# Layer two's weights converted earlier, and bits hashed in four row groups, in a hash attention and two-layer feed-forward kernel

## The chip, the cores and the metric

The kernel runs on one core of a Trainium2 chip. Its time is the device time of one execution in microseconds (us). The engines are TensorE (PE in the profile; its weight loads are PEld), VectorE (DVE), ScalarE (ACT), GpSimd (POOL) and SyncE (SP), which here issues every transfer. They run at the same time and wait for each other through semaphores; each takes its own instructions strictly in the order in which they were written out when the kernel was built.

## What is computed

Attention in which a query sees only keys of its own bucket, then two feed-forward layers on the result:

```python
q_bits = (einsum('bhsd,dk->bhsk', q, proj) > 0)          # 6 bits, k_bits likewise
mask = q_bucket[:, :, :, None] == k_bucket[:, :, None, :]
scores = where(mask, q @ k.T / sqrt(D), -1e9)            # B 2, H 8, S 768, D 64
x = softmax(scores) @ v                                  # as 1536 tokens of 512
x = relu(x @ w_in)**2 @ w_out                            # layer one, 512 -> 2048 -> 512
h = x @ w_in2
out = (max(h, 0) + alpha * min(h, 0)) @ w_out2           # layer two
```

The four weight matrices come as float64, and reach the core as pairs of 32-bit words.

## The kernel before

The 1536 tokens are cut into four chunks (c = 0 to 3) of 384. A chunk's attention is four pairs of heads; a pair is six units (two heads by three blocks of 128 queries). Layer one runs `feed_forward(0, c)` and layer two `feed_forward(1, c)`, each over 16 blocks f of the hidden width. Attention of chunk 0 runs alone at the start; attention of chunk c + 1 is cut into steps that a `Background` object hands out between the matmuls of `feed_forward(0, c)` by a table of marks, so that it is done 0.8 of a chunk after chunk c began. Chunk 3 of layer one has no attention beside it.

*Weights.* A unit u = (layer, f, o) is one 128x512 block of the input (o = 0) or output (o = 1) weights. `load_bits` brings its 512 KB of words from DRAM (tile wbits). `to_f32` makes float32 of them with one ACT instruction (line 444, tile we) and three on DVE (446 and 447 to wsg, 448 to the result). `split_w` then splits a float32 block into a high part (wh, ACT, line 462) and the rest (wl, line 463, on DVE or POOL), and the matmuls use both. Layer one's 32 units are converted in `fetch`, and written to DRAM (`w_d`), during `feed_forward(0, 0)` and a little before; chunks 1 to 3 load them back as 256 KB each (tile wf, line 488). Layer two's 32 units are converted by `keep` into a pool that stays (`res`), by a `Background` whose marks spread them from the start of chunk 3 of layer one to 0.3 of the first chunk of layer two.

*Bits.* `hash_bits` multiplies a pair's keys (768 columns) or queries (384) by the projection, 128 columns wide, with float32 matmuls (line 214), and DVE takes the sign into tile bits (215). `matches` multiplies these by a table of +1 and -1 (`code`, line 227), so that equal buckets can be told from the sums.

*Key halves.* `k_split` rounds each head's 64 rows of keys to the matmul format on ACT (236), writes the remainder to the other 64 rows on DVE (237) and copies the rounded part to a second tile on POOL (238).

*Evictions.* `p_t` transposes the exponentials and copies them out of PSUM, 3 by 128 columns at a time, on ACT ("a", line 317) or DVE ("v", line 319) by the strings in `EVICT`, one per chunk. `scores` has the score matmuls (292, 293), a maximum on DVE (`low`, 296) and the exponential on ACT (`sm`, 299).

A scheduler writes out each engine's order at build time from the program's order and its own idea of durations; pools with one or two buffers decide what must wait for what.

## Time and profile before

| | |
|---|---|
| median of three runs | 870.07 us (867.12 to 870.68) |
| the profiled execution | 869.21 us, of which its span 867.4 us |
| mean granted TensorE clock | 0.985 of full speed |
| busy share: PE, DVE, ACT, POOL | 93%, 64%, 55%, 44% |
| moved by DMA | 96.40 MB |

The span runs from the first instruction to the last; 1.8 us lie around it. A busy PE can still be waiting inside an instruction, so its share says little by itself: what counts is the time that a stage takes against the matmuls it has to do. The stages follow from the copies of the chunk results out of PSUM: attention 0 runs to about 91 us (first matmul of layer one at 90.88), chunk 0 to 246, chunk 1 to 377, chunk 2 to 491, chunk 3 to 588, and the four chunks of layer two take 69 us each, and the last writes out its result.

### The profile page before, as it was taken

How to read it: one execution, taken by the hardware profiler on the slowest of the kernel's cores; microseconds unless marked ns; L12 is line 12 of the kernel's file. 1: busy time of each engine (PE TensorE's matmuls, PEld its weight loads, DVE VectorE, ACT ScalarE, POOL GpSimd, SP SyncE). 2: the span in 40 equal slices, each digit the busy share in tenths (PEclk: the TensorE clock that was granted, in tenths of full speed). 3: DMA queues.
4: the chain of work that ended last, by engine and by line, in shares of the span. 5: the costliest groups of instructions: out<-in, count | busy, mean ns of one | idle time of the engine just before them, and what ended most of it. 6: DMA issues, size and time to landing. Idle time of an engine off the chain costs nothing.

```text
span 867.4 us, 12076 instructions
## 1 busy us (share of the span) xinstructions
PE 810.9 (93%) x4192; PEld 653.4 (75%) x4192; DVE 552.7 (64%) x854; ACT 480.6 (55%) x925; POOL 378.6 (44%) x328
## 2 busy tenths in 40 slices
PE   5998998899999999999999998868999999999996
PEld 3655677676768778778777877647998998998995
DVE  6989899997666345366454599978445444444442
ACT  5668668776656556557555656654444444444331
POOL 3011233432646556433332554475555555554553
PEclk7999999999999999999999999989999999999999
DMA  7442766664332233342223777750010010000000
GB/s 232 139 133 96 254 183 210 223 203 133 112 129 71 88 110 80 89 126 85 71 82 88 274 234 259 262 215 37 1 37 37 0 38 37 1 1 37 1 0 37
DMA packets 42989, 96.40 MB, mean 111 GB/s; under 512 B 5200, under 2 KB 13744, under 8 KB 42928
## 3 DMA queue, kind: packets, MB, share of 16 engines
q1 hardware_dynamic: 42928, 95.63, 34.2%
q8 instruction: 33, 0.54, 0.3%
q14 instruction: 28, 0.23, 0.1%
HBM read 80.88 MB, written 14.73 MB: 110 GB/s over the span
## 4 chain that ended last, share of the span: by engine, by line
PE 59%; DVE 9%; issue 4%; ACT 3%; DMA 3%; POOL 2%; SPq 0%; POOLq 0%; DVEq 0%; ACTq 0%
PE acc L542 8%; PE acc L538 7%; PE acc L539 7%; PE m L329 5%; PE h L510 4%; PE h L512 4%; PE h L511 4%; PE m L313 4%; PE m L512 3%; PE m L510 3%; PE m L511 3%; PE s L292 2%; PE s L293 2%; DVE wsg L447 2%; DVE wl L463 2%
## 5 line engine op out<-in xcount | busy, mean ns | idle before, releaser
L528 POOL TENSOR_TENSOR gl<-g,gh 128x384 fp32r<-128x384 f32 x128 | 142.6, 1114 | 266.3 <-ACT gh L527 122.2
L538 PE MATMUL acc<-wh,gh 128*128 128x512 f32 x384 | 162.0, 422 | 12.6 <-ACT gh L519 10.2
L463 POOL TENSOR_TENSOR wl<-wf,wh 128x512 fp32r<-128x512 f32 x80 | 107.7, 1347 | 119.3 <-ACT wh L462 109.0
L539 PE MATMUL acc<-wl,gh 128*128 128x512 f32 x384 | 152.2, 396 | 0.0
L542 PE MATMUL acc<-wh,gl 128*128 128x512 f32 x384 | 117.2, 404 | 9.0 <-POOL gl L528 8.9
L462 ACT ACTIVATE wh<-w 128x512 fp32r<-128x512 f32 x128 | 80.4, 629 | 74.8 <-PE m L511 40.3
L462 ACT ACTIVATE wh<-wf 128x512 fp32r<-128x512 f32 x128 | 79.5, 627 | 56.0 <-PE h L511 28.9
L510 PE MATMUL h<-xh,wh 128*128 128x384 f32 x296 | 107.2, 362 | 1.1 <-ACT xh L357 0.8
L511 PE MATMUL h<-xl,wh 128*128 128x384 f32 x296 | 101.0, 341 | 0.6 <-POOL xl L358 0.6
L512 PE MATMUL h<-xh,wl 128*128 128x384 f32 x296 | 101.2, 342 | 0.0
L296 DVE TENSOR_REDUCE low<-s 128x1 f32<-128x768 f32 x84 | 80.1, 954 | 29.4 <-PE s L293 28.7
L538 PEld LDWEIGHTS acc<-wh,gh 128*128 128x128 f32 x384 | 72.6, 189 | 31.1 <-ACT gh L519 13.0
L542 PEld LDWEIGHTS acc<-wh,gl 128*128 128x128 f32 x384 | 71.9, 190 | 30.8 <-POOL gl L528 15.2
L299 ACT ACTIVATE sm<-s,low 128x768 f32<-128x768 f32 x84 | 75.3, 896 | 27.4 <-DVE low L296 27.1
L313 PE MATMUL m<-ident,sm 128*128 128x128 f32 x528 | 83.0, 274 | 5.8 <-DVE bits L215 4.0
L463 POOL TENSOR_TENSOR wl<-w,wh 128x512 fp32r<-128x512 f32 x64 | 83.9, 1310 | 8.9 <-ACT wh L462 8.6
L313 PEld LDWEIGHTS m<-ident,sm 128*128 128x128 f32 x528 | 65.5, 140 | 21.8 <-DVE bits L215 4.9
L539 PEld LDWEIGHTS acc<-wl,gh 128*128 128x128 f32 x384 | 72.9, 190 | 9.7 <-issue 1.2
L527 ACT ACTIVATE gh<-g 128x384 fp32r<-128x384 f32 x64 | 33.5, 524 | 83.6 <-DVE g L526 83.6
L525 DVE TENSOR_SCALAR r<-m,alpha_sb 128x384 f32<-128x384 f32 x43 | 26.5, 617 | 82.3 <-PE m L512 82.1
L319 DVE COPY pt<-m 128x384 f32<-128x384 f32 x112 | 61.4, 552 | 23.3 <-PE m L313 23.0
L512 PE MATMUL m<-xh,wl 128*128 128x384 f32 x216 | 72.9, 338 | 0.5 <-DVE wl L463 0.5
(105 smaller groups left out, 1568.6 us busy)
## 6 DMA issues: line engine op xcount, KB each, us to landing
wf<-w SPq DMA_DIRECT2D x96, 256.0 KB
wbits<-in_w_in_dram SPq DMA_DIRECT2D x32, 512.0 KB
wbits<-in_w_out_dram SPq DMA_DIRECT2D x32, 512.0 KB
w<-wf SPq DMA_DIRECT2D x32, 256.0 KB
qr<-in_qT_dram SPq DMA_DIRECT2D x32, 192.0 KB
kr<-in_kT_dram SPq DMA_DIRECT2D x8, 384.0 KB
qn<-in_qT_dram SPq DMA_DIRECT2D x16, 192.0 KB
vr<-in_v_dram SPq DMA_DIRECT2D x8, 384.0 KB
```

The lines of the kernel that those rows point to most:

```text
L296: nc.vector.tensor_reduce(low, ps[:, 0:2, 0:HALF], AX.XY, ALU.max, negate=True)
L299: nc.scalar.activation(sm.rearrange("p (a n) -> p a n", a=2), ps[:, 0:2, 0:HALF], AF.Exp, bias=low, accum_out=self.sums[:, i:i + 1],)
L313: nc.tensor.transpose(ps[:, i * P:(i + 1) * P], pp[:, b * P:(b + 1) * P], ident)
L462: nc.scalar.activation(hi, w, AF.Copy)
L463: engine.tensor_tensor(lo, w, f32(hi), ALU.subtract)
L510: nc.tensor.matmul(hp, wih[:, ks], xh[:, kk, :], start=first, stop=False)
L511: nc.tensor.matmul(hp, wih[:, ks], xl[:, kk, :], start=False, stop=False)
L512: nc.tensor.matmul(hp, wil[:, ks], xh[:, kk, :], start=False, stop=last)
L528: nc.gpsimd.tensor_tensor(gl, g, f32(gh), ALU.subtract)
L538: nc.tensor.matmul(acc[:, t, :], gh[:, blocks[t]], woh, start=first, stop=False)
L539: nc.tensor.matmul(acc[:, t, :], gh[:, blocks[t]], wol, start=False, stop=False)
L542: nc.tensor.matmul(acc[:, t, :], gl[:, blocks[t]], woh, start=False, stop=last)
```

## The change

Four edits come together.

*Layer two's conversion.* Its units are now converted in chunks 1 and 2 of layer one, by steps handed out from 1.0 to 2.9, beside the attention steps: `ahead` converts a unit in place in the tile we and stores it to DRAM. `keep` becomes a load of 256 KB from there, from 0.25 of chunk 3 to 0.3 of layer two's first chunk. The tiles we and wsg have one buffer in place of two in the later stage, and the tile pool of wf outlives the attention.

*Bits.* The projection keeps 16 columns per head (32 in all). `hash_bits` cuts the columns of keys or queries into four parts and multiplies each into its own group of 32 PSUM partitions, so DVE takes signs of 192 columns for keys and 96 for queries. `matches` uses one table per group, four matmuls and four weight loads per call. The tables take some more small instructions at the start.

*Key halves.* Except for the very first pair, POOL subtracts in place in the key tile, and two transfers per head move the rounded part to the second tile and the remainder to the other 64 rows.

*Evictions.* Chunk 0 and chunk 1 have one more "a" per head each, two per pair.

```diff
-EVICT = ("avavav", "vvavva", "vvavva", "vvavva")
+EVICT = ("aavaav", "avavav", "vvavva", "vvavva")
...
-        state["conv"] = pool(f"conv{late}", 1 + late, stack)
+        state["conv"] = pool(f"conv{late}", 1, stack)
...
+    GR = 32
+    NG = P // GR
-    proj_sb = const.tile([P, P], F32, name="proj_sb")
+    proj_sb = const.tile([P, 2, GR // 2], F32, name="proj_sb")
-    code = const.tile([P, P], BF16, name="code")
+    code = const.tile([P, NG, P], BF16, name="code")
...
         def hash_bits(self, x, n):
+            w = n // NG
+            bits = p1.tile([P, S // NG], BF16, tag="bits", name="bits")[:, 0:w]
+            ps = m_tile()
+            for g in range(NG):
+                nc.tensor.matmul(
+                    ps[g * GR:(g + 1) * GR, 0:w], proj_sb.rearrange("p h n -> p (h n)"), x[:, g * w:(g + 1) * w],
+                    start=True, stop=True,
+                )
+            nc.vector.tensor_scalar(bits, ps[:, 0:w], 0.0, None, ALU.is_gt)
+            return bits
...
-            for a in range(n // T):
-                nc.tensor.matmul(ps[:, a, 0:T], code, bits[:, a * T:(a + 1) * T], start=True, stop=True)
+            for g in range(NG):
+                a, k = divmod(g * w, T)
+                nc.tensor.matmul(ps[:, a, k:k + w], code[:, g, :], bits, start=True, stop=True)
...
+            shift = self.c > 0 or self.j > 0
             for h in range(2):
                 r, o = self.rows(h)
                 nc.scalar.activation(self.k1[r, h], self.kr[r], AF.Copy)
-                nc.vector.tensor_tensor(self.k1[o, h], self.kr[r], f32(self.k1[r, h]), ALU.subtract)
-                nc.gpsimd.tensor_copy(self.k2[r, h], f32(self.k1[r, h]))
+                if shift:
+                    nc.gpsimd.tensor_tensor(
+                        self.kr[r].bitcast(F32R), self.kr[r], f32(self.k1[r, h]), ALU.subtract
+                    )
+                    nc.sync.dma_start(out=f32(self.k2[r, h]), in_=f32(self.k1[r, h]))
+                    nc.sync.dma_start(out=f32(self.k1[o, h]), in_=self.kr[r])
...
+    def ahead(u):
+        w = to_f32(u)
+        w_d[u] = dram.tile([P, DM], F32, tag="w%d_%d_%d" % u, name="w%d_%d_%d" % u)
+        nc.sync.dma_start(out=w_d[u], in_=w)
+
     def keep(u):
         kept[u] = state["res"].tile([P, DM], F32, name="w%d_%d_%d" % u)
-        to_f32(u, kept[u])
+        nc.sync.dma_start(out=kept[u], in_=w_d[u])
...
+    for f in range(KFF):
+        for o in range(2):
+            steps += [lambda u=(1, f, o): load_bits(u), lambda u=(1, f, o): ahead(u)]
+    conversion = Background(steps, [(1.0, 0), (NCH - 1.1, len(steps))])
...
     steps = [lambda f=f, o=o: keep((1, f, o)) for f in range(KFF) for o in range(2)]
-    conversion = Background(steps, [(0.0, 0), (1.3, len(steps))])
+    conversion = Background(steps, [(0.25, 0), (1.3, len(steps))])
```

How the written order moves is shown at three places. Names end in a number that tells tiles apart; an arrow points from what is read to what is written.

DVE in chunk 3 of layer one, before (446 to 448 convert layer two's units, 463 splits a unit of layer one):

```order
L448 SCALAR_TENSOR_TENSOR w1_2_0_5528<-we_5531,wsg_5533 128x512
L446 TENSOR_SCALAR wsg_5551<-wbits_5547 128x512
L447 SCALAR_TENSOR_TENSOR wsg_5551<-wbits_5547,wsg_5551 128x512
L448 SCALAR_TENSOR_TENSOR w1_2_1_5546<-we_5549,wsg_5551 128x512
L463 TENSOR_TENSOR wl0_5607<-wf_5584,wh0_5606 128x512
L446 TENSOR_SCALAR wsg_5595<-wbits_5591 128x512
L447 SCALAR_TENSOR_TENSOR wsg_5595<-wbits_5591,wsg_5595 128x512
L448 SCALAR_TENSOR_TENSOR w1_3_0_5590<-we_5593,wsg_5595 128x512
```

DVE at the end of chunk 2 and in chunk 3, in the changed kernel (496 is the split, 556 the square of the hidden value, 625 the chunk's copy out, 652 part of the next layer's input):

```order
L556 TENSOR_TENSOR g_5709<-r_5708 128x384
L556 TENSOR_TENSOR g_5759<-r_5758 128x384
L625 COPY y_5788<-acc_4548 128x512 x2
L496 TENSOR_TENSOR wl0_5819<-wf_5766,wh0_5818 128x512
L496 TENSOR_TENSOR wl0_5852<-wf_5847,wh0_5851 128x512
L496 TENSOR_TENSOR wl0_5895<-wf_5880,wh0_5894 128x512
L652 TENSOR_TENSOR xl_6060<-s_6118,xh_6059 128x4x128
L496 TENSOR_TENSOR wl0_5937<-wf_5923,wh0_5936 128x512
```

None of the 29 conversions that stood in chunk 3 is left there.

DVE in chunk 1, before (a pair's reciprocals, evictions and signs):

```order
L341 RECIPROCAL rin_3794<-rin_3794 128x6
L319 COPY pt_3712<-m_3775 128x384
L319 COPY pt_3712<-m_3782 128x384
L345 COPY rrow_3799<-m_3797 6x128
L356 TENSOR_TENSOR x_3859<-u_3839,rb_3803 128x384
L215 TENSOR_SCALAR bits_3876<-m_3877 128x384
L296 TENSOR_REDUCE low_3901<-s_3896 128x1
L215 TENSOR_SCALAR bits_3935<-m_3936 128x384
```

and in the changed kernel, around the same work (471, 472 and 474 convert; 321 is the maximum, 344 the eviction, 232 the signs):

```order
L370 COPY rrow_3362<-m_3360 6x128
L474 SCALAR_TENSOR_TENSOR we_3773<-we_3773,wsg_3775 128x512
L471 TENSOR_SCALAR wsg_3864<-wbits_3820 128x512
L472 SCALAR_TENSOR_TENSOR wsg_3864<-wbits_3820,wsg_3864 128x512
L381 TENSOR_TENSOR x_3559<-u_3410,rb_3366 128x384
L321 TENSOR_REDUCE low_3417<-s_3412 128x1
L232 TENSOR_SCALAR bits_3440<-m_3441 128x192
L344 COPY pt_3451<-m_3452 128x384
L344 COPY pt_3451<-m_3459 128x384
L474 SCALAR_TENSOR_TENSOR we_3862<-we_3862,wsg_3864 128x512
L321 TENSOR_REDUCE low_3469<-s_3464 128x1
L471 TENSOR_SCALAR wsg_3958<-wbits_3915 128x512
```

Of the conversions, 2 now stand before chunk 0's copy out, 22 in chunk 1 and 8 in chunk 2 (counted by line 474).

SP in chunk 1, before, with what each transfer waits for in brackets (488 loads a unit of layer one; DMAHW is an earlier transfer on the same semaphore):

```order
L347 DMA rin0_2832<-rrow_2830 6x128 [waits DMAHW3_49,DVE_49]
L350 DMA rb_2834<-rin0_2832 64x384 [waits DMAHW4_49,DMAHW3_49]
L350 DMA rb_2834<-rin0_2832 64x384 [waits DMAHW5_49]
L488 DMA wf_2978<-w0_5_1_1311 128x512 [waits DMAHW6_49,Pool_49]
L488 DMA wf_3071<-w0_6_0_1417 128x512 [waits DMAHW7_49,Pool_49]
L488 DMA wf_3073<-w0_6_1_1426 128x512 [waits DMAHW2_49,DMAHW0_49,Pool_49]
```

and in the changed kernel (521 loads a unit of layer one, 483 stores a converted one, 459 loads words, 260 moves a key remainder):

```order
L521 DMA wf_3120<-w0_5_0_1376 128x512 [waits DMAHW0_49,Pool_49]
L483 DMA w1_2_0_3292<-we_3286 128x512 [waits DMAHW1_49,DVE_49]
L459 DMA wbits_3548<-in_w_out2_dram 128x1024 [waits DMAHW2_49,Activation_49]
L521 DMA wf_3122<-w0_5_1_1385 128x512 [waits Pool_49]
L260 DMA k1_3068<-kr_2841 64x768 [waits DMAHW4_49,Pool_49]
L260 DMA k1_3068<-kr_2841 64x768 [waits DMAHW5_49,Pool_49]
L483 DMA w1_2_1_3389<-we_3383 128x512 [waits DMAHW6_49,DVE_49]
L459 DMA wbits_3624<-in_w_in2_dram 128x1024 [waits DMAHW7_49,Activation_49]
```

Stores that wait for DVE and key transfers that wait for POOL now stand between the loads; chunk 1 has 104 transfers between the two chunk results on SP, where it had 56.

## Rows read from the trace of the kernel before

**Rows 1.** Windows by stage: us, then busy per engine (instructions), clock, DMA share, GB/s.
```profile
0.00:91.00 91.00, 75.43 (x378) 47.51 (x379) 78.61 (x130) 58.52 (x112) 14.30 (x21) 0.94 0.47 152
91.00:246.00 155.00, 144.34 (x774) 111.60 (x774) 134.65 (x206) 111.17 (x219) 58.78 (x50) 0.99 0.58 184
246.00:377.00 131.00, 129.44 (x709) 99.59 (x707) 66.39 (x101) 75.32 (x154) 69.46 (x64) 1.00 0.32 94
377.00:491.00 114.00, 113.73 (x624) 89.12 (x622) 55.40 (x95) 61.65 (x127) 40.73 (x36) 1.00 0.38 115
491.00:588.00 97.00, 78.42 (x362) 65.16 (x361) 88.52 (x113) 61.09 (x119) 51.02 (x33) 0.95 0.69 237
588.00:657.00 69.00, 66.29 (x333) 58.62 (x332) 37.53 (x60) 28.67 (x52) 36.41 (x32) 1.00 0.06 22
657.00:726.00 69.00, 68.65 (x350) 61.66 (x349) 31.42 (x53) 29.53 (x53) 36.47 (x33) 1.00 0.07 24
```

**Rows 2.** Waits of PE in 491 to 588: total us, times, longest.
```profile
PE acc L538 <- ACT gh L519: 10.2, 8, 2.8
PE acc L542 <- POOL gl L528: 7.5, 3, 7.0
```

**Rows 3.** Lines, 491 to 588, the conversions: count, busy us, mean ns, idle before.
```profile
L448 DVE SCALAR_TENSOR_TENSOR w<-we,wsg 128x512 uint32<-128x512 uint32 x29 | 28.8, 995 | 1.9
L447 DVE SCALAR_TENSOR_TENSOR wsg<-wbits,wsg 128x512 uint32<-128x512 uint32 x29 | 26.0, 903 | 0.6
L446 DVE TENSOR_SCALAR wsg<-wbits 128x512 uint32<-128x512 uint32 x29 | 16.9, 588 | 0.1
L444 ACT ACTIVATE we<-wbits 128x512 f32<-128x512 f32 x31 | 20.8, 671 | 27.8 <-DMA wbits<-in_w_in_dram 13.5 <-DVE w L448 7.6 <-DMA wbits<-in_w_out_dram 6.4
```

**Rows 4.** Timeline of POOL, DVE and PE from 570 us: start, us, instruction, idle before.
```profile
570.60 8.14 POOL L528 TENSOR_TENSOR gl<-g,gh 128x384 fp32r<-128x384 f32 x1 [3.70 <-ACT g L521]
572.93 1.28 DVE L447 SCALAR_TENSOR_TENSOR wsg<-wbits,wsg 128x512 uint32<-128x512 uint32 x2
578.80 0.80 PE L542 MATMUL acc<-wh,gl 128*128 128x512 f32 x1 [6.98 <-POOL gl L528]
```

**Rows 5.** Lines of POOL, 491 to 588 first, then 246 to 377.
```profile
L528 POOL TENSOR_TENSOR gl<-g,gh 128x384 fp32r<-128x384 f32 x16 | 26.5, 1654 | 39.7 <-ACT g L521 32.3 <-DMA wbits<-in_w_in_dram 4.2 <-DMA wf<-w 3.3
L528 POOL TENSOR_TENSOR gl<-g,gh 128x384 fp32r<-128x384 f32 x16 | 16.4, 1024 | 1.0
L463 POOL TENSOR_TENSOR wl<-wf,wh 128x512 fp32r<-128x512 f32 x29 | 37.8, 1302 | 42.5 <-ACT wh L462 41.3 <-PE s L293 1.0 <-PE m L313 0.2
```

**Rows 6.** Waits of the DMA queue of SP, 246 to 491.
```profile
SPq L488 <- POOL wl L463: 129.4, 40, 7.3
```

**Rows 7.** Lines of DVE, 0 to 246.
```profile
L319 DVE COPY pt<-m 128x384 f32<-128x384 f32 x54 | 29.3, 549 | 1.1 <-PE m L313 0.9
L448 DVE SCALAR_TENSOR_TENSOR wf<-we,wsg 128x512 uint32<-128x512 uint32 x32 | 25.2, 788 | 3.2 <-POOL wl L463 1.8 <-DMA rb<-rin 0.2 <-DVE wsg L447 0.2
L447 DVE SCALAR_TENSOR_TENSOR wsg<-wbits,wsg 128x512 uint32<-128x512 uint32 x32 | 24.1, 754 | 0.5
L446 DVE TENSOR_SCALAR wsg<-wbits 128x512 uint32<-128x512 uint32 x32 | 18.4, 577 | 0.5
L237 DVE TENSOR_TENSOR k<-kr,k 64x768 fp32r<-64x768 f32 x16 | 18.1, 1131 | 5.3 <-ACT k L236 4.8
L215 DVE TENSOR_SCALAR bits<-s 128x768 bf16<-128x768 f32 x6 | 5.7, 953 | 2.9 <-PE s L214 2.8
L215 DVE TENSOR_SCALAR bits<-m 128x384 bf16<-128x384 f32 x9 | 4.9, 544 | 0.0
```

**Rows 8.** Lines of ACT over the whole span.
```profile
L317 ACT ACTIVATE pt<-m 128x384 f32<-128x384 f32 x64 | 30.9, 484 | 6.3 <-PE m L313 6.2
```

**Rows 9.** Timeline of PE: one key hash, then eight matmuls on column halves.
```profile
215.84 1.45 PE L214 MATMUL s<-kr,proj_sb 128*128 128x384 f32 x4
470.42 1.51 PE L329 MATMUL m<-pt,vr 128*64 128x384 f32 x8
```

More of the change, by code (lines that the diff above doesn't have):

```diff
@@ L77 @@
     m2 = pool("m2", 2)
+    state_whole = pool("whole", 4)
     weights = ctx.enter_context(ExitStack())
     att = ctx.enter_context(ExitStack())
-    state = {"attention": True, "moe": False, "s": 0, "m": 0, "h": 0}
+    state = {"attention": True, "moe": False, "s": 0, "m": 0, "h": 0, "whole": state_whole}
     def weight_pools(stack, late):
-        if not late:
-            state["whole"] = pool("whole", 4, stack)
-        state["conv"] = pool(f"conv{late}", 1 + late, stack)
+        state["conv"] = pool(f"conv{late}", 1, stack)
         state["parts0"] = pool(f"parts0{late}", 2 + late, stack)
@@ L134, in constants @@
         with tc.tile_pool(name="once", bufs=1) as once:
-            cols = once.tile([P, 2, D], i32, name="cols")
+            cols = once.tile([P, D], i32, name="cols")
             row = once.tile([P, 1], i32, name="row")
+            bit = once.tile([P, 1], i32, name="bit")
             nb = once.tile([P, 2, NB], i32, name="nb")
+            part = once.tile([P, 2 * NG], i32, name="part")
+            of = once.tile([P, 2 * NG], F32, name="of")
+            sign = once.tile([P, D], F32, name="sign")
             nc.gpsimd.iota(row, [[0, 1]], base=0, channel_multiplier=1)
-            nc.gpsimd.iota(cols, [[0, 2], [1, D]], base=0, channel_multiplier=0)
+            nc.gpsimd.iota(cols, [[1, D]], base=0, channel_multiplier=0)
+            nc.gpsimd.iota(part, [[-GR // 2, 2 * NG]], base=0, channel_multiplier=1)
             nc.gpsimd.iota(nb[:, 0, :], [[0, NB]], base=0, channel_multiplier=1)
             nc.gpsimd.iota(nb[:, 1, :], [[1, NB]], base=0, channel_multiplier=0)
-            nc.vector.tensor_scalar(row, row, 31, None, ALU.bitwise_and)
-            nc.vector.tensor_scalar(cols, cols, row, 1, ALU.logical_shift_right, ALU.bitwise_and)
-            nc.vector.tensor_scalar(
-                code.rearrange("p (h n) -> p h n", h=2), cols, 2.0, -1.0, ALU.mult, ALU.add
-            )
-            for h in range(2):
-                nc.vector.memset(code[h * D:(h + 1) * D, h * D:(h + 1) * D], 0.0)
+            nc.vector.tensor_copy(of, part)
+            above = once.tile([P, 2 * NG], F32, name="above")
+            nc.vector.tensor_scalar(above, of, 0.0, None, ALU.is_ge)
+            nc.vector.tensor_scalar(of, of, float(GR // 2), None, ALU.is_lt)
+            nc.vector.tensor_tensor(of, of, above, ALU.mult)
+            nc.vector.tensor_scalar(bit, row, GR // 2 - 1, None, ALU.bitwise_and)
+            nc.vector.tensor_scalar(cols, cols, bit, 1, ALU.logical_shift_right, ALU.bitwise_and)
+            nc.vector.tensor_scalar(sign, cols, 2.0, -1.0, ALU.mult, ALU.add)
+            for g in range(NG):
+                for h in range(2):
+                    nc.vector.tensor_scalar(
+                        code[:, g, (1 - h) * D:(2 - h) * D], sign, of[:, 2 * g + h:2 * g + h + 1], None, ALU.mult
+                    )
             nc.vector.tensor_tensor(nb[:, 0, :], nb[:, 0, :], nb[:, 1, :], ALU.logical_shift_right)
@@ L212, in hash_bits @@
                 ps = m_tile().unsqueeze(1)
-            for a in range(n // T):
-                nc.tensor.matmul(ps[:, a, 0:T], proj_sb, x[:, a * T:(a + 1) * T], start=True, stop=True)
-            nc.vector.tensor_scalar(
-                bits.rearrange("p (a n) -> p a n", n=T), ps[:, 0:n // T, 0:T], 0.0, None, ALU.is_gt
-            )
-            return bits
-        def matches(self, bits, n):
-            if n > T:
-                ps = s_tile()
-            else:
-                ps = m_tile().unsqueeze(1)
-            for a in range(n // T):
-                nc.tensor.matmul(ps[:, a, 0:T], code, bits[:, a * T:(a + 1) * T], start=True, stop=True)
+            for g in range(NG):
+                a, k = divmod(g * w, T)
+                nc.tensor.matmul(ps[:, a, k:k + w], code[:, g, :], bits, start=True, stop=True)
             return ps[:, 0:n // T, 0:T]
@@ L447, in to_f32 @@
         nc.vector.scalar_tensor_tensor(s, t[:, :, 0], 29, s, ALU.logical_shift_right, ALU.bitwise_or)
+        w = e if w is None else w
         nc.vector.scalar_tensor_tensor(
@@ L637, with beside @@
     following = Background(steps, marks)
+    steps = []
+    for f in range(KFF):
+        for o in range(2):
+            steps += [lambda u=(1, f, o): load_bits(u), lambda u=(1, f, o): ahead(u)]
+    conversion = Background(steps, [(1.0, 0), (NCH - 1.1, len(steps))])
+    def beside(x):
+        following(x)
+        conversion(x)
     for c in range(NCH - 1):
-        feed_forward(0, c, lambda x: following(c + x))
+        feed_forward(0, c, lambda x: beside(c + x))
+    conversion(NCH)
     following(NCH)
```

14 lines of the change are left out of this document (11 added, 3 removed).

## The prediction

> **What bounds the kernel now.** I read the stages first, then the waits and the instruction groups inside the one stage that stands out. [rows 1] has one line per stage. A layer-two chunk is 350 matmuls in 69 us, with PE busy for 68.7 of them: that is the price of a feed-forward chunk when nothing else is in its way. Chunk 3 of layer one has the same matmuls plus a dozen transposes, and takes 97 us, with DVE busy for 88.5. So about 28 us there are not TensorE's work. The same comparison dates the other stages: chunk 2 has 624 - 350 = 274 matmuls of attention in 114 - 69 = 45 us, 0.164 us each; chunk 1 has 359 in 62 us, 0.173; chunk 0 has 424 in 155 - 69 = 86 us, 0.203. At chunk 2's rate chunk 0 has lost 424 x 0.039 = 16.5 us, and chunk 1 three. Chunks 1 and 2 have PE busy for 99% of their time and are TensorE's; attention 0 (DVE 78.6 of 91) and chunk 0 (134.7 of 155) lean on DVE.
>
> Inside chunk 3 the three DVE steps of 29 conversions take 28.8 + 26.0 + 16.9 = 71.7 us, their ACT step 20.8, and ACT sits 27.8 us in front of that step, mostly until words land or until DVE has let go of a buffer [rows 3]. PE waits there for ACT's and POOL's parts of the hidden value [rows 2], which are queued behind those conversions.
>
> **Chunk 3: -25 us.** All 29 conversions leave it. DVE keeps 88.5 - 71.7 = 17 us of work, ACT 61 - 21 = 40, POOL 51, in a stage that PE needs 69 us for. Each conversion is replaced by a load of 256 KB instead of 512 KB. The stage moved 237 GB/s x 97 us = 23.0 MB [rows 1]; less 29 x 0.26 that is 15.4 MB, or 65 us at the same rate, so transfers are late only if they run slower than now. I take 72 us: 69 and three for the first blocks, whose loads meet at the start. The ends are 69 us (-28) and 84 us (-13), which is 15.4 MB at the 184 GB/s of the stage of chunk 0. The first chunk of layer two loses its last three conversions and with them about the 2 us by which PE is less busy there than a chunk later: -2, between 0 and -2.4.
>
> **Attention 0 and chunk 0: -9 and -6 us.** From DVE go, at the means of [rows 7]: 16 evictions of 0.549 (8 in each stage); 13 of the 15 subtractions that stood there, at the 0.954 us that most take (their mean of 1.131 holds two long ones): 6 in attention 0, 7 in chunk 0; and most of the signs. Those fall on a line through 953 ns for 768 columns and 544 ns for 384, which gives 340 ns for 192 and 240 ns for 96: 0.61 us off per key call (six) and 0.30 per query call (nine). Attention 0 so loses 4.4 + 5.7 + 3.6 = 13.7 us of DVE and gains some ten small instructions for the tables, near 1.6 us: 12 net of 78.6. Chunk 0 loses 4.4 + 6.7 + 2.7 = 13.8 and takes in two or three early conversions at 788 + 754 + 577 = 2.12 us, 5.3 in all: 8.5 net of 134.7. ACT pays 8 x 0.484 = 3.9 us in each [rows 8], and has 32 and 44 us free. I take three quarters of DVE's relief in attention 0, where nothing else is near its limit, and a little less in chunk 0. The ends are the whole relief (-12 and -8.5, with chunk 0 reaching -12 if its lost 16.5 us shrink faster than DVE's load) and nothing, or +3 in attention 0 if its keys come late: a subtraction on POOL should take 1.9 us, by the line through 1024 ns for 384 columns and 1302 for 512 [rows 5], and a transfer follows it. POOL is idle for 77 of those 91 us and a pair's keys are prepared three units ahead, some 10 us at 91 / 24 a unit, which hides it; without that cover each of three pairs would cost the 4 us by which its keys are later.
>
> **The hash on TensorE: -2 us.** Four full-width matmuls take 1.45 us; eight on column halves, of the same 384 columns, take 1.51 [rows 9], so two halves do run side by side. Eight on quarters, of 192 columns, should take between a half and a quarter of that: about 0.7 us off per key call. Four such calls lie in chunks 0 and 1. A query call saves about 0.3 us and pays it back in three more weight loads in `matches`. The ends are 0 and -4.
>
> **Chunks 1 and 2: +12 us.** Here 22 and 8 conversions come in: at 2.12 us each 47 us of DVE into chunk 1, which has 65 free, and 17 into chunk 2, which has 59. On ACT it is 0.67 each, 15 and 5 us, with 56 and 52 free. The work fits; what it costs is delay for the maximum, eviction and split behind it in the same order. Where conversions stand among attention and feed-forward now, chunk 0 loses 16.5 us with 24 of them, 0.69 each if it is all theirs; in chunk 3 it is 28 / 29 = 0.97 each. The ends are thus 0 and 29 us. I take 0.4 each, nearer chunk 0 than nothing: no matmul soon waits for these units, and DVE's fill will be some 85% in chunk 1, as in chunk 0, but 64% in chunk 2.
>
> **Sum.** -25 - 2 - 9 - 6 - 2 + 12 = -32. The profiled span of 867.4 becomes 835.4, and with 1.8 us around it 837.2; that execution (869.21) is 0.9 below the median of the three. I predict 837.
>
> **Rivals.**
>
> *The middle chunks pay chunk 3's price: 854.* 30 x 0.97 = 29 us instead of 12. For it: POOL's part of the hidden value took 8.14 us once, where 1.02 is usual, while DVE ran one conversion step after another, and PE waited 6.98 us for it [rows 4]; its mean in chunk 3 is 1654 ns against 1024 in chunk 1 [rows 5], where POOL has most to do (69.5 us) and gets key subtractions besides. The Trainium skill, GPSIMD Engine Reference, Specifications, says that VectorE and GpSimd share SBUF interfaces and that VectorE instructions with two SBUF inputs, or in a two-port mode, contend for them. By that rule the conversions hold POOL up wherever they are put, and this rival is the result; the trace agrees as far as the one long instruction shows. Against it: with one buffer, conversions can't run in a row for long; other DVE work stands between them.
>
> *One buffer and one queue: 873, slower than before.* The next unit's ACT step must wait until the store of the one before has landed, since both use we; that store is issued by SP, which in chunks 1 and 2 already stands 129.4 us, in 40 waits of up to 7.3, before loads whose buffer POOL has not freed [rows 6]. Behind the waiting ACT step stand splits, evictions and exponentials. Such a wait is 3.2 us on the mean; if half of it, 1.6 us per conversion, reaches PE, 30 of them cost 48 instead of 12. The kernel becomes slower than before from (32 + 12) / 30 = 1.47 us per conversion. Against it: ACT has 40% of these chunks free, and the scheduler puts the step where it thinks the store done.
>
> *The front does not move: 852.* Attention 0 and chunk 0 are bound by the chain from score to maximum to exponential to transposes and not by DVE's fill, or keys come late; the 15 us stay. For it: PE's share there is 83% and 93% without long waits on DVE. Against it: DVE's 86% and 87%.
>
> *All of DVE's relief counts and the middle is free: 818.* -12 and -12 in front, and 5 of the 12 us.
>
> **Chances.** The forecast, 828 to 846: 0.50. Chunk 3's price: 0.20. Front unmoved: 0.10. All relief: 0.12. One buffer: 0.08. The kernel before can't be told from a time within 0.5%, 865.7 to 874.4. The first four are below it, but the second and third together, or a dearer second, can come in there or above: I put 0.03 within and 0.01 above for that. One buffer at its price or less gives 0.02 within, and more gives 0.06 above. So faster 0.88, same 0.05, slower 0.07. The range for 8 in 10, 818 to 860, leaves out the rest of these two and the lower tail of the fourth.
>
> **What would show it.** Chunk 3 about 72 us long with PE busy almost throughout and no conversion on DVE; a layer-two chunk unchanged at 69. Chunk 1 near 140 us and chunk 2 near 116, DVE at 80 to 85% and 65%. First matmul of layer one near 82 us instead of 91. ACT's waits before its conversion step under 1 us each. Key hashes of about 0.7 us. Wrong, if chunk 1 is over 155 us, if chunk 3 stays above 84, or if ACT's waits for the store exceed 1.5 us per unit.

## The result and the profile after

The changed kernel takes 860.8 us (median of 4; 859.8 to 862.2) against 868.7 for the one before in the same comparison: a ratio of 0.990, 95% interval 0.988 to 0.992. It is faster, by 8 us and not by the 33 that were forecast, and lies just above the range's upper end of 860. The profiled execution is the longest of the four (862.2 us, of which its span 860.2).

Windows by stage, cut at the same places as [rows 1] (the last result copy of a chunk; for the first, where layer one's matmuls run on); busy times in the order PE, PEld, DVE, ACT, POOL:

```profile
0.00:95.30 95.30, 75.28 (x438) 49.09 (x438) 72.81 (x133) 61.88 (x121) 19.46 (x22) 0.95 0.61 188
95.30:245.40 150.10, 140.89 (x828) 108.21 (x826) 120.22 (x192) 112.22 (x224) 56.02 (x43) 0.98 0.68 215
245.40:394.50 149.10, 133.46 (x768) 101.40 (x768) 114.58 (x165) 89.80 (x179) 86.82 (x70) 0.99 0.65 204
394.50:511.40 116.90, 114.73 (x642) 88.73 (x640) 70.86 (x120) 66.13 (x135) 42.72 (x36) 1.00 0.48 156
511.40:581.30 69.90, 68.67 (x347) 61.56 (x346) 16.49 (x24) 43.87 (x87) 37.21 (x33) 1.00 0.59 202
581.30:650.70 69.40, 69.06 (x353) 62.23 (x352) 30.30 (x55) 30.06 (x53) 36.34 (x33) 1.00 0.07 26
```

Chunk 3 went from 96 us to 69.9 and the chunk after it from 70.9 to 69.4: what the forecast built on came, and VectorE has 16.5 us of work where it had 88. The gain was lost ahead of that. Chunk 1 has grown from 131 us to 149.1, with TensorE busy for 133 of them where it was busy throughout, and chunk 2 by 2.7; the first attention took 95.3 us, not 82, though VectorE works 72.8 us there and no longer 78.6 (the sign that the forecast named, the first matmul of layer one, stands at 89.20, the second at 95.80). Chunk 0 is 4.3 us shorter.

The hash is as forecast. PE's timeline has a key hash as eight matmuls in 0.53 us, where [rows 9] had 1.45:

```profile
262.74 0.53 PE L228 MATMUL m<-kr,proj_sb 128*32 128x192 f32 x8
```

The conversions' lines on VectorE in chunk 1 (count | busy us, mean ns | idle before):

```profile
L472 DVE SCALAR_TENSOR_TENSOR wsg<-wbits,wsg 128x512 uint32<-128x512 uint32 x21 | 22.5, 1070 | 0.6
L474 DVE SCALAR_TENSOR_TENSOR we<-we,wsg 128x512 uint32<-128x512 uint32 x22 | 20.7, 939 | 22.4 <-ACT we L469 22.2
L471 DVE TENSOR_SCALAR wsg<-wbits 128x512 uint32<-128x512 uint32 x21 | 11.9, 566 | 0.4
```

A unit costs VectorE 1.07 + 0.94 + 0.57 = 2.58 us here, against the 2.12 of [rows 7] and the 2.49 of [rows 3]. The waits of chunk 1 (who for whom: us, times, longest), ScalarE's first, then TensorE's:

```profile
ACT we L469 <- DMA w<-we: 21.7, 11, 4.5
ACT sm L324 <- DVE low L321: 9.2, 14, 2.1
...
PE s L244 <- ACT sm L324: 5.0, 2, 3.4
```

ScalarE stands 21.7 us before its conversion step, 1.0 us per unit, until a store has landed; before, TensorE had no wait of over 1 us in this chunk, and none for the exponential. The timeline from 265 us shows the two joined:

```profile
265.56 1.60 DVE L474 SCALAR_TENSOR_TENSOR we<-we,wsg 128x512 uint32<-128x512 uint32 x1
...
266.64 3.93 SPq L260 DMA_DIRECT2D k<-kr  x2
...
268.10 1.96 POOL L256 TENSOR_TENSOR kr<-kr,k 64x768 fp32r<-64x768 f32 x1
...
270.66 0.54 SPq L483 DMA_DIRECT2D w<-we  x1
...
271.00 0.94 DVE L321 TENSOR_REDUCE low<-s 128x1 f32<-128x768 f32 x1
...
273.89 0.66 ACT L469 ACTIVATE we<-wbits 128x512 f32<-128x512 f32 x1 [3.55 <-DMA w<-we]
...
274.87 0.88 ACT L324 ACTIVATE sm<-s,low 128x768 f32<-128x768 f32 x1
...
275.90 0.49 PE L244 MATMUL s<-bits,code 128*128 128x192 bf16 x4 [3.37 <-ACT sm L324]
```

VectorE has a converted unit ready at 267.16. SyncE issues its store only at 270.66: until then it stands at a key transfer (line 260), which waits for GpSimd's subtraction of 268.10 to 270.06. The next unit's ScalarE step waits for that store until 273.89. The exponential stands behind it until 274.87, though its maximum is ready at 271.94, and TensorE waits 3.37 us for the score tile. That is the rival of one buffer and one queue, at work. The experiments ask how much of the 18 us it is.

### The profile page after: what moved, and what is told of

Same layout as the page of the kernel before. It is cut to its first block, busy times and chain, and to the rows that moved or that the text cites. A ratio compares the mean times of both kernels' runs of the same rounds, so it can differ in the third digit from the quotient of the medians.

```text
span 860.2 us, 12647 instructions
## 1 busy us (share of the span) xinstructions
PE 804.5 (94%) x4384; PEld 652.2 (76%) x4384; DVE 515.6 (60%) x834; ACT 487.4 (57%) x941; POOL 385.7 (45%) x329
## 4 chain that ended last, share of the span: by engine, by line
PE 55%; DVE 10%; DMA 6%; ACT 4%; issue 4%; POOL 2%; SPq 0%; POOLq 0%; DVEq 0%; ACTq 0%
PE acc L575 8%; PE acc L571 7%; PE acc L572 7%; PE m L545 4%; PE m L543 4%; PE m L544 4%; PE m L354 4%; PE h L543 4%; DMA w<-we 4%; PE h L544 4%; PE h L545 3%; DVE low L321 2%; PE m L338 1%; PE s L317 1%; DVE we L474 1%
## 5 line engine op out<-in xcount | busy, mean ns | idle before, releaser
L561 POOL TENSOR_TENSOR gl<-g,gh 128x384 fp32r<-128x384 f32 x128 | 136.5, 1066 | 244.8 <-ACT gh L560 123.0
L571 PE MATMUL acc<-wh,gh 128*128 128x512 f32 x384 | 160.0, 417 | 0.0
L575 PE MATMUL acc<-wh,gl 128*128 128x512 f32 x384 | 115.4, 399 | 1.8 <-POOL gl L561 1.8
L338 PE MATMUL m<-ident,sm 128*128 128x128 f32 x525 | 84.9, 279 | 3.9 <-DVE pt L344 1.4
L572 PEld LDWEIGHTS acc<-wl,gh 128*128 128x128 f32 x384 | 72.8, 189 | 9.8 <-issue 1.8
L317 PE MATMUL s<-k,q 128*128 128x384 f32 x168 | 64.4, 383 | 16.0 <-ACT sm L324 13.5
```

Source lines behind the costliest of these rows:

```text
L338: nc.tensor.transpose(ps[:, i * P:(i + 1) * P], pp[:, b * P:(b + 1) * P], ident)
L561: nc.gpsimd.tensor_tensor(gl, g, f32(gh), ALU.subtract)
L571: nc.tensor.matmul(acc[:, t, :], gh[:, blocks[t]], woh, start=first, stop=False)
L572: nc.tensor.matmul(acc[:, t, :], gh[:, blocks[t]], wol, start=False, stop=False)
L575: nc.tensor.matmul(acc[:, t, :], gl[:, blocks[t]], woh, start=False, stop=last)
```

## The experiments

All of one table: median, ratio to the kernel before in the same comparison with its interval, and the stages of the profiled execution in us. A stage is that of one execution, which lies up to 4 us from its run's median (e2: 860.9 against 865.1), so a difference of a few us between two runs' stages says little by itself.

| run | us | ratio (95%) | att. 0 | chunk 0 | chunk 1 | chunk 2 |
|---|---|---|---|---|---|---|
| before | 868.7 | 1 | 91.2 | 154.4 | 131.2 | 114.2 |
| after | 860.8 | 0.990 (0.988-0.992) | 95.3 | 150.1 | 149.1 | 116.9 |
| e1 | 859.3 | 0.988 (0.985-0.990) | 91.0 | 152.2 | 149.5 | 116.2 |
| e2 | 865.1 | 0.995 (0.993-0.997) | 92.1 | 148.3 | 129.8 | 114.3 |
| e3 | 864.0 | 0.992 (0.990-0.995) | 92.8 | 151.9 | 155.6 | 113.8 |
| e4 | 847.9 | 0.974 (0.972-0.976) | 90.3 | 154.4 | 136.3 | 117.1 |
| e5 | 862.0 | 0.992 (0.989-0.995) | 92.1 | 151.2 | 147.6 | 118.4 |
| e6 | 863.4 | 0.992 (0.990-0.995) | 91.3 | 151.2 | 155.6 | 113.1 |
| e7 | 859.4 | 0.988 (0.987-0.990) | 92.8 | 148.7 | 153.5 | 114.3 |
| e8 | 854.3 | 0.982 (0.981-0.984) | 94.8 | 154.2 | 138.6 | 117.9 |
| e9 | 857.1 | 0.985 (0.982-0.988) | 90.5 | 156.3 | 139.8 | 117.8 |
| e10 | 848.5 | 0.976 (0.972-0.979) | 94.2 | 145.3 | 145.2 | 117.6 |
| e11 | 855.2 | 0.983 (0.980-0.985) | 92.7 | 151.3 | 144.4 | 117.7 |
| e12 | 849.5 | 0.977 (0.974-0.980) | 92.5 | 147.3 | 143.3 | 115.1 |
| e13 | 862.4 | 0.992 (0.989-0.995) | 92.6 | 158.3 | 148.5 | 115.5 |
| e14 | 861.9 | 0.992 (0.989-0.994) | 90.3 | 149.5 | 129.9 | 114.3 |
| e15 | 848.7 | 0.976 (0.973-0.979) | 91.3 | 154.8 | 138.2 | 116.5 |
| e16 | 850.0 | 0.978 (0.975-0.980) | 89.1 | 155.2 | 138.5 | 117.4 |
| e17 | 861.7 | 0.992 (0.989-0.995) | 91.8 | 150.2 | 154.6 | 114.3 |
| e18 | 853.9 | 0.982 (0.979-0.985) | 90.4 | 154.8 | 144.8 | 114.3 |

### The parts apart: e1, e2, e4, e14

e1 is the kernel before with the moved conversion alone (`ahead`, `keep`, the marks and pools of the change).

> The kernel before with one part of the change: layer two's weights converted in chunks 1 and 2 and kept by way of DRAM; hash, key halves and EVICT as before. Theory A (the conversions themselves make chunk 1 longer, through the one buffer we): chunk 1 near 148 us, as in the changed kernel, attention 0 near 91, chunk 0 near 154, chunk 3 near 70, in all about 862. Theory B (the key halves on GpSimd and their transfers make chunk 1 longer): chunk 1 near 135, in all about 849. On attention 0 both say 91.

Measured 859.3, chunk 1 at 149.5: the conversion alone makes chunk 1 as long as the whole change does. Theory A, on this run.

e2 is the changed kernel with the conversion put back; its edit is e1's, the other way.

> The changed kernel without the moved conversion: hash in four row groups, key halves by GpSimd and transfers, EVICT as changed; layer two's weights converted in chunk 3 as before. Theory A: chunk 1 near 130 us, chunk 3 near 97, attention 0 near 95 and chunk 0 near 150 as in the changed kernel, in all about 866. Theory B: chunk 1 near 143, in all about 879.

Measured 865.1, chunk 1 at 129.8: without conversions in that chunk the key part costs it nothing. Windows of its attention 0, chunk 0 and chunk 1:

```profile
0.00:92.10 92.10, 71.73 (x439) 45.98 (x439) 71.28 (x131) 61.45 (x121) 19.47 (x22) 1.00 0.62 189
92.10:240.40 148.30, 137.89 (x828) 105.89 (x826) 115.47 (x185) 110.24 (x221) 54.98 (x43) 1.00 0.63 199
240.40:370.20 129.80, 128.64 (x766) 99.89 (x767) 61.66 (x100) 76.96 (x157) 79.19 (x70) 1.00 0.36 101
```

e4 puts the key halves back:

```
-            shift = self.c > 0 or self.j > 0
+            shift = False
```

> The changed kernel with the key halves made as before for all pairs (subtraction on VectorE, copy on GpSimd); the rest as changed. If late keys are what the first attention lost: attention 0 falls from 95 us to 91 or less and chunk 0 rises by 2 to 4. If it is the evictions given to ACT or the longer tables at the start: attention 0 stays at 94 to 96, and chunk 0 rises by the same 2 to 4, in all 861 to 864. Theory B on chunk 1: it falls by 10 us or more; theory A: by less than 3.

Measured 847.9, 13 us under the changed kernel and the lowest of the table (e10 and e15 can't be told from it); chunk 1 falls by 12.8 us, for theory B. So neither theory holds alone: the key part costs nothing without conversions (e2) and 13 us with them. Windows of e4, attention 0 to chunk 3:

```profile
0.00:90.30 90.30, 70.74 (x439) 46.16 (x440) 77.43 (x139) 63.24 (x123) 13.92 (x22) 1.00 0.56 180
90.30:244.60 154.30, 141.67 (x837) 109.08 (x836) 136.24 (x203) 113.51 (x228) 59.76 (x50) 0.99 0.61 199
244.60:380.90 136.30, 128.96 (x758) 98.42 (x757) 105.91 (x160) 86.40 (x173) 76.22 (x64) 1.00 0.64 200
380.90:498.00 117.10, 115.18 (x645) 88.88 (x643) 70.51 (x121) 66.59 (x135) 42.62 (x36) 1.00 0.50 162
498.00:568.00 70.00, 68.79 (x347) 61.68 (x347) 16.51 (x24) 43.95 (x87) 37.13 (x33) 1.00 0.59 203
```

e14 has the edits of e2 and e4 both: hash and evictions alone.

> Hash in four groups and EVICT as changed, keys as before, weights converted in chunk 3 as before. With the key part this made 865.1 us. If the key part costs something only where conversions stand beside it: 862 to 866. If it costs its 9 to 13 us anywhere: 852 to 856.

Measured 861.9. This closes the account. From before to e14, hash and evictions: -0.85%. From e14 to e4, the conversion: -1.7%. From e4 to the changed kernel, the key part: +1.6% (each about 0.3 either way). Of 870 us that is -7.4, -15.1 and +13.8. Without conversions the key part (e14 to e2) is +0.3%, at the edge of the noise, or 2.8 us, and the conversion added last (e2 to the changed kernel) is -0.5%, or -4.0. So the split depends on the order in which the parts are added: 11 us belong to neither part alone but to the two together.

### Which half of the key part: e9, e10, e13, e5

e9 subtracts on GpSimd straight into k1, with no transfers; e10 keeps the transfers and subtracts on VectorE:

```
e9:  (nc.gpsimd if shift else nc.vector).tensor_tensor(self.k1[o, h], ...)
     nc.gpsimd.tensor_copy(self.k2[r, h], ...)
e10: nc.vector.tensor_tensor(self.kr[r].bitcast(F32R), ...)   # was nc.gpsimd; both dma_starts stay
```

> The changed kernel without the key transfers: GpSimd subtracts straight into k1 and copies the high half into k2, as VectorE and GpSimd did before; VectorE makes no key half. If the transfers are the cost (SyncE's order, theory A2): attention 0 near 91 us, chunk 1 near 138, in all about 849. If GpSimd's load is the cost (theory K: the keys come late, and what GpSimd runs holds VectorE's conversion steps up): chunk 1 at 148 or more, in all 860 or more.

> The changed kernel with VectorE doing the key subtractions and the transfers as changed. Theory A2: the transfers still stand in SyncE's order, but no longer wait for GpSimd; chunk 1 is between 140 and 146 us, in all 852 to 857. Theory K: chunk 1 falls to about 137, in all 848 to 850.

By whole times the subtraction on GpSimd costs 9 us (857.1) and the transfers 1 (848.5): theory K. By single stages it is less clear, since e10's chunk 0 is 9 us shorter than e4's and its chunk 1 9 longer: the units between them shift. Chunks 0 and 1 together agree with the whole times: 290.6 us in e4, 290.5 in e10, 296.1 in e9, 299.2 in the changed kernel.

One more thing differs between these runs, the place of the subtractions. In e9 all fourteen on GpSimd stand ahead of chunk 1, which starts at 246.8; this is the last:

```profile
240.45 2.17 POOL L256 TENSOR_TENSOR k<-kr,k 64x768 fp32r<-64x768 f32 x1
```

Subtracted in place, they come behind the hash that reads the same tile, and four of them, of two pairs, fall into chunk 1: at 264.76, at 268.10 and two from 301.24 on in the changed kernel, and likewise in e10 on VectorE. So e9's 9 us are not a meeting of subtractions and conversions in chunk 1, which is 139.8 us long there.

e13 adds the subtraction to e4 in place, after the last reader of kr, for all pairs but the first:

```
+ nc.gpsimd.tensor_tensor(self.kr[r].bitcast(F32R), self.kr[r], f32(self.k1[r, h]), ALU.subtract)
```

> The kernel with the keys on VectorE (847.9 us), and on GpSimd the changed kernel's subtraction once more, in place, with no reader: GpSimd has the load of the run with subtraction on GpSimd and no transfers (857.1 us), but no key waits for it. Theory G (it is GpSimd's load that costs: it runs beside VectorE and holds conversion steps up, and its own later work is late): 855 to 859. Theory K (the keys come late, and what needs them waits): 847 to 850.

Measured 862.4, above the 855 to 859 expected: the subtractions on GpSimd cost the whole 14 us with nobody waiting for their result. Late keys aren't needed for the price, and no wait of TensorE in the first attention and chunks 0 and 1 of the changed kernel names a key transfer. Windows of chunks 0 and 1:

```profile
92.60:251.00 158.40, 143.14 (x837) 110.53 (x837) 138.90 (x203) 113.86 (x228) 68.82 (x54) 0.98 0.60 194
251.00:399.40 148.40, 132.92 (x760) 100.58 (x758) 113.84 (x163) 88.16 (x175) 82.95 (x68) 0.98 0.62 194
```

And what TensorE waited for there (timeline from 310 us):

```profile
310.22 0.38 SPq L463 DMA_DIRECT2D wbits<-in_w_in_dram  x1
...
310.70 0.38 SPq L487 DMA_DIRECT2D w<-we  x1
...
311.69 0.94 DVE L325 TENSOR_REDUCE low<-s 128x1 f32<-128x768 f32 x1
...
316.13 0.66 ACT L473 ACTIVATE we<-wbits 128x512 f32<-128x512 f32 x1 [4.31 <-DMA w<-we]
...
317.11 0.88 ACT L328 ACTIVATE sm<-s,low 128x768 f32<-128x768 f32 x1
...
318.13 0.80 PE L244 MATMUL s<-bits,code 128*128 128x192 bf16 x4 [4.40 <-ACT sm L328]
```

The maximum is ready at 312.6; ScalarE stands before its conversion step until 316.1, when the store issued at 310.70 has landed (a load of 512 KB had been issued just ahead of it, at 310.22), and the exponential starts at 317.1. This one wait is the picture of the changed kernel without any key transfer.

Of chunk 1 TensorE is idle for 15.5 us here (148.4 less 132.9) and 15.6 in the changed kernel, against 7.3 in e4: 8 of the 12 or 13 us are waits. The other 4 are longer busy time for about as many matmuls. Some of it is the granted clock, which was lower right behind the long waits: 0.72 after the one of 3.37 us in the changed kernel, 0.50, near 1.2 GHz, after the one of 4.40 us in e13. First the changed kernel, then e13:

```profile
276.00:282.00 6.00, 6.00 (x36) 5.18 (x35) 4.20 (x7) 2.58 (x5) 1.73 (x3) 0.72 0.67 228
318.00:324.00 6.00, 5.87 (x27) 4.95 (x27) 4.24 (x6) 1.88 (x4) 1.65 (x2) 0.50 0.54 168
```

What this run can't separate: the order is the same as e4's in attention 0 and chunk 0 but for the added instructions and a swap of two loads, yet in chunk 1 the scheduler put ScalarE's and VectorE's conversion steps at other places among the exponentials and maxima, as it did in the changed kernel. Attention 0 and chunk 0, with their order kept, lost 2 and 4 us; the 12 of chunk 1 are load and order together.

e5 issues both key transfers by `nc.gpsimd.dma_start`.

> The changed kernel with the two transfers per key half issued by GpSimd and not by SyncE, so that SyncE's order no longer stands before them. Theory A2 (in chunk 1 SyncE waits for GpSimd's subtraction before a key transfer, the store of a converted unit stands behind it, ScalarE's next conversion step waits for that store in the one buffer, and the exponentials wait behind ScalarE): ScalarE's waits before the conversion step fall from 21.7 us to about 10, as with the keys on VectorE, chunk 1 from 149 us to about 138, in all about 850. Rival D (GpSimd's subtractions themselves, or their hold on VectorE, make chunk 1 long): chunk 1 stays at 147 to 150, in all 859 to 862.

Measured 862.0, chunk 1 at 147.6: taking the key transfers out of SyncE's order gave nothing back, so theory A2 fails here. GpSimd pays for the issuing, though (0.56 us each, the last at 302.88); e9, which has no key transfers at all, still costs 9 us. Timeline from 303 us:

```profile
303.38 7.07 DVE L474 SCALAR_TENSOR_TENSOR we<-we,wsg 128x512 uint32<-128x512 uint32 x1 [0.66 <-ACT we L469]
303.46 1.03 POOL L561 TENSOR_TENSOR gl<-g,gh 128x384 fp32r<-128x384 f32 x1
...
308.92 0.98 POOL L561 TENSOR_TENSOR gl<-g,gh 128x384 fp32r<-128x384 f32 x1
...
310.38 0.94 DVE L321 TENSOR_REDUCE low<-s 128x1 f32<-128x768 f32 x1
...
311.36 0.90 ACT L324 ACTIVATE sm<-s,low 128x768 f32<-128x768 f32 x1 [6.70 <-DVE low L321]
...
312.40 0.80 PE L244 MATMUL s<-bits,code 128*128 128x192 bf16 x4 [6.38 <-ACT sm L324]
```

One conversion step lasted 7.07 us where the shortest take 0.7: it began at 303.38, GpSimd ran six instructions in a row from 303.46 to 309.9, and the step ended at 310.4. The Trainium skill, SBUF — State Buffer, SBUF: two separate sides, says that GpSimd and a VectorE instruction with two SBUF inputs take a shared pair of ports by an exclusive lock: the one that starts first holds it for its whole instruction, and the other is blocked. These rows fit a VectorE shut out, but over six instructions, not one, and the profile has its step begin 0.08 us ahead of the first of them. On the mean it is small: a unit takes VectorE 2.58 us in the changed kernel's chunk 1 and 0.89 + 0.79 + 0.82 = 2.51 in e4's; in e5's it takes 3.05.

In e5 that one step did reach TensorE: the maximum stands behind it on VectorE, the exponential behind the maximum, and the next matching of bits waits 6.38 us. The same place in e4:

```profile
303.72 0.49 PE L244 MATMUL s<-bits,code 128*128 128x192 bf16 x4 [1.33 <-ACT sm L324]
```

This bears on what e13 leaves open. In chunk 1 ScalarE and VectorE of e5 have the order of e4 but for a few places, most of them at its start, and yet the chunk is 11.3 us longer, 5 of them by this wait. So GpSimd's load (subtractions and issuing) costs here without a new order on those two engines.

### The wait for the store: e3, e6, e7, e17, e18, e12

e3 writes the result over the words; e6 gives wsg two buffers and puts the result there; e7 is e6 with e4's edit:

```
e3: w = t.rearrange("p n b -> p (n b)")[:, 0:DM].bitcast(F32) if w is None else w
e6: e = t[:, :, 1].bitcast(F32)          # ScalarE's step in place; conv pool of 2
    w = s.bitcast(F32) if w is None else w
```

> The changed kernel; the conversion's last step writes its result over the words it came from (tile wbits, three buffers) and not over we, so that the next unit's ACT step no longer waits for the store of the unit before. Theory A (one buffer): ACT's waits before its conversion step, 21.7 us in chunk 1, go to under 3; chunk 1 falls from 149 us to about 135, in all about 847. Rival C (the conversions fill DVE, or hold GpSimd up, wherever their result goes): chunk 1 stays at 146 to 149, in all 858 to 861.

> The changed kernel with two buffers for what is stored: ScalarE writes its step over the words it read, and the result is put over wsg, which gets a second buffer; the memory is the same, and ScalarE's step waits for VectorE's first step but for no store. Theory A2: ScalarE's waits for stores go to nothing and chunk 1 falls from 149 us to 138 or less, in all 849 or less. Rival D: chunk 1 stays above 146, in all above 857.

> Two buffers as in the run before, and the key halves made by VectorE and GpSimd as before the change. Theory A2: the 10.2 us that ScalarE still waits for stores with the keys on VectorE go too, and chunk 1 falls from 136 us to 132 or so, in all about 843. Rival C (what is left in chunk 1 is VectorE's fill): chunk 1 stays at 136, in all 847 to 849.

Measured 864.0, 863.4 and 859.4, chunk 1 at 154 to 156 in all three: worse. The wait changed hands. In e6 ScalarE waits longer than before, for VectorE's first step:

```profile
ACT wbits L471 <- DVE wsg L469: 27.5, 14, 4.3
```

With more buffers the scheduler also moved more units from chunk 2 into chunk 1 (25 in e3 and e6, 27 in e7, 21 in the changed kernel), so these runs are no clean test of the buffer.

e17 leaves the stores out and lets layer two load layer one's weights; e18 is e17 with e4's edit:

```
-        nc.sync.dma_start(out=w_d[u], in_=w)
+        w_d[u] = w_d[0, u[1], u[2]]
```

> The changed kernel without the stores of layer two's converted weights: they are converted as before and thrown away, and layer two loads layer one's weights from DRAM in their place, so that layer two's result is not the reference's. All 29 conversions left after chunk 0 then stand in chunk 1 or at its edge, since nothing holds them back. Theory A2 (ScalarE's wait for the store, with exponentials behind it, is most of the price): chunks 1 and 2 together fall from 266 us to 255 or less, in all 850 or less. Rivals C and G (VectorE's work and GpSimd beside it): 262 to 267 together, in all 857 to 862.

> The same without stores, with the keys on VectorE (847.9 us with stores; chunks 1 and 2 together 253 us). If the waits for stores are what the key part made worse, this and the run before meet within 4 us in all. If the key part costs by GpSimd's load alone, they stay 10 us or more apart.

Measured 861.7 and 853.9; chunks 1 and 2 together 268.9 and 259.1. Without any store to wait for, ScalarE stands as long, now until VectorE has let go of the one buffer:

```profile
ACT we L469 <- DVE we L474: 19.8, 12, 2.6
```

Theory A2 isn't borne out: the store is only the last of the things that a ScalarE step waits for. The test has a flaw of its own, since 26 units stand in chunk 1 of e17 where the changed kernel has 21; chunks 1 and 2 together, which hold nearly the same units in both, took 268.9 us against 266.0. The key part still costs 8 us, between the 4 and the 10 that were to decide.

e12 leaves out two of VectorE's three steps:

```
+        if w is None:
+            nc.vector.tensor_scalar(e, e, 8.0, None, ALU.mult)
+            return e
```

> The changed kernel with two of VectorE's three conversion steps left out for layer two's weights, and the third a multiplication of we alone, so that those weights are not the reference's; loads, ScalarE's step and stores stay. Theory C (VectorE's work is the price): chunk 1 falls from 149 us to about 133, chunk 2 to 114, in all about 841. Theory A2 (waits for stores and SyncE's order): chunk 1 stays at 142 or more, in all 851 or more.

Measured 849.5, chunk 1 at 143.3, between the two. Its window and ScalarE's wait:

```profile
239.80:383.10 143.30, 132.49 (x766) 101.33 (x767) 70.98 (x122) 89.23 (x177) 79.55 (x70) 0.99 0.69 212
```

```profile
ACT we L469 <- DMA w<-we: 19.4, 11, 3.4
```

VectorE has 44 us less to do than in the changed kernel and the chunk is still 13 longer than in e2. Of the 19 us that conversions cost the changed kernel there (149.1 against 129.8), 6 went with two of VectorE's three steps; the rest is there with ScalarE's step, one step of VectorE, loads and stores.

### Smaller questions: e8, e11, e15, e16

e8 is e4 with the key hash in the score tile (`ps = s_tile()[:, 0, :] if n > T else m_tile()`); e11 and e15 set `SQUARE = "aava"` in the changed kernel and in e4; e16 is e4 with the EVICT of before.

> The kernel with the keys on VectorE (847.9 us), but the key hash put into the score tile s, as before the change, and not into a tile m; it is still four row groups. Theory S (with conversions in the way, the one score tile is what chunk 1 runs out of, and the key hash of before held it some 3 us per pair; this is why the conversion alone had chunk 1 at 149.5 us): chunk 1 rises from 136 us to 143 or more, in all 855 or more. Rival: it is the shorter hash on TensorE and the shorter signs on VectorE: chunk 1 stays at 136 to 138, in all 848 to 850.

Measured 854.3, 6 us slower, but chunk 1 only 2 longer, and attention 0 4.5: a tile of its own for the key hash is worth something, though not where theory S had it. It leaves open why e1, with the wide hash and without the key part, needs 149.5 us for chunk 1 and e4 136.3.

> The changed kernel with the square of chunk 1 (16 instructions of 0.95 us on GpSimd) moved to ScalarE, so that GpSimd has 15 us less to do in chunk 1. Theory G (GpSimd running back to back holds up VectorE's conversion steps, one of which took 7.07 us beside six GpSimd instructions in a row): the conversion steps in chunk 1 get shorter, 2.58 us per unit to 2.3 or less, and chunk 1 falls by 5 us or more, to 144 or less, in all 856 or less. Rival: it stays within 2 us of 149, since ScalarE pays 8 us more.

> The kernel with the keys on VectorE (847.9 us) and the square of chunk 1 on ScalarE. If GpSimd's load is what conversions suffer from, less of it helps here too: 843 to 846. If only the key subtractions were too much: 847 to 850.

e11: 855.2, chunk 1 down 4.7, with 2.44 us of VectorE per unit where theory G wanted 2.3 or less; e15: 848.7, no change against e4. Load taken off GpSimd helped only where the key subtractions stand on it.

> The kernel with the keys on VectorE (847.9 us) and the evictions dealt out as before the change (16 more on VectorE, 8 in attention 0 and 8 in chunk 0). If VectorE's relief counts as forecast: attention 0 and chunk 0 longer by 3 us each, 853 to 855 in all. If attention 0 isn't bound by VectorE's load: attention 0 unchanged at 90 to 92, 847 to 851 in all.

Measured 850.0, some 2 us over e4 and at the edge of the noise. Attention 0, with ScalarE's eight evictions given back to VectorE, takes 89.1 us:

```profile
0.00:89.10 89.10, 70.76 (x439) 45.65 (x439) 75.71 (x141) 59.26 (x112) 13.52 (x22) 1.00 0.50 157
```

## Why the prediction was wrong

*Chunk 3 (-25) and layer two's first chunk (-2): right.* -26.1 and -1.5; 69.9 us is the 69 of a chunk with nothing in its way plus one, as the forecast's lower end had it.

*The hash (-2): right.* 0.53 us per key hash against about 0.7; chunk 1 of e14 and e2 is 1.3 us shorter than before, with two of the four calls in it; in chunk 0 the hash can't be told from the evictions.

*Conversions in chunks 1 and 2 (+12): near with the new hash and the old keys, too low otherwise.* With keys on VectorE they cost 136.3 + 117.1 - 129.9 - 114.3 = 9.2 us, 0.3 each for 28 units; with the key part (the changed kernel less e2) 21.9, 0.75 each for 29. Without the key part but with the wide hash (e1 less before) they cost 20.3, so the key part is not the only thing that raises their price, and what the hash has to do with it stays open. The whole move of the conversion, -25 - 2 + 12 with the 3.7 by which the forecast let early ones eat into chunk 0's relief, stood at -11; e14 to e4 gave -15. In e1 it gave -10.9, by luck: chunk 0 got 2.2 us shorter there and not longer.

*Attention 0 (-9): wrong.* The step that failed is "I take three quarters of DVE's relief in attention 0, where nothing else is near its limit". VectorE's work there was 78.8, 77.4, 75.7 and 71.3 us in before, e4, e16 and e2, and the stage took 91.2, 90.3, 89.1 and 92.1: it does not follow. VectorE was fullest, but its fill is not what ended the stage. The rival "the front does not move" had this right, for attention 0 alone; chunk 0 gave 4.3 of the 6. Of the 95.3 us in the profiled execution of the changed kernel some 3 are the clock's (below): e2 runs the same attention 0 in 92.1.

*The key part: the step that failed most.* Split by part, the forecast's -32 held about -9 for it: 5.7 us of subtractions off VectorE in attention 0 and 6.7 in chunk 0, counted at the shares that the forecast took of all relief there, 0.75 and 0.7, are -4.3 and -4.7. GpSimd's side was entered as nothing, "POOL is idle for 77 of those 91 us ... which hides it", for attention 0 alone; chunk 1, where conversions and four subtractions of two pairs meet, got no term. Measured +13.8 beside conversions. The difference, 23 us, is as large as the whole miss of 24; hash and evictions (-7.4 for about -12) and the conversion (-15 for -11) miss by 4 either way. In the other order of the parts the key part misses by 12 (+2.8), the conversion by 7 (-4.0) and hash and evictions by the same 4: either way 11 us are the price of the two together, for which the forecast had no term. GpSimd's subtraction itself was sized right (1.87 us in chunk 1 for 1.9).

*The rivals.* "One buffer and one queue" describes what stands on the timeline, and its mark, over 1.5 us per unit, wasn't reached: 1.0. Taking the store away (e17) gave nothing back. "Chunk 3's price" named the meeting of conversions and key subtractions on two engines and came nearest with 854. Its time is near in part by luck: it has chunks 1 and 2 at +29 where the changed kernel has +21 against before, and the front at -15 where it has -0.2. The sum of the last rival, 818, is off: its own terms, 9 us more in front and 5 in place of 12, give 821. Nothing else hangs on it.

Shown: the subtractions on GpSimd, in the order that the scheduler then writes, bring the whole price beside conversions with nobody waiting for their result (e13), and without key transfers most of it (e9); late keys, SyncE's order (e5) and the store (e17) aren't needed for it. A new order on ScalarE and VectorE isn't needed either, as e5 shows, where 5 us of chunk 1 are one VectorE step that lasted beside GpSimd's instructions. Not shown: how the price of the changed kernel, whose order in chunk 1 is e13's and not e4's, divides between such steps and the place of ScalarE's conversion step in front of an exponential. ScalarE's wait for the store isn't the measure: from the changed kernel to e4 it fell with the price, from 21.7 to 10.2 us in chunk 1, but e13 has 11.4 and e1 10.9, and both have a chunk 1 as long as the changed kernel's. The rows of e4, e13 and e1:

```profile
ACT we L469 <- DMA w<-we: 10.2, 8, 2.5
ACT we L473 <- DMA w<-we: 11.4, 7, 4.3
ACT we L443 <- DMA w<-we: 10.9, 7, 2.5
```

## What to carry to other kernels

Price a move with the load on the engine that receives it, in the stage where the other parts of the same change land: the key part cost 0.3% alone and 1.6% beside conversions, and the conversion brought 1.7% without it and 0.5% with it. An engine's fill named no bound here: count relief only where the waits show something standing behind that engine. See where the new form lets an instruction stand: in place, four subtractions moved behind a hash and into the stage that the conversions moved to. And run a change of several parts in parts; here the version without one part (847.9) beats both kernels.
